# A spectral filter and a low-rank mixer: batch 0's spectra made twice against one filter tile, and its loads reordered

## The chip, the cores and the metric

The kernel runs on one core of one Trainium2 chip. The metric is the time of one execution in device microseconds (us); the time of a kernel is the median of its runs. A profile is one execution taken by the hardware profiler. The engines are PE (matrix multiply, with its weight loads shown as PEld), DVE (vector engine), ACT (scalar engine), POOL (GpSimd) and SP, which here only issues transfers. Transfers issued by POOL can change the number type on the way (x and the filters are float32 in memory and float16 on the core), those issued by SP and ACT do not here.

## What is computed

```python
X = np.fft.rfft(x, axis=1)                  # x: 8 batches, 3136 rows, 256 columns
Y = X * (filt_r + 1j * filt_i)[None]        # 1569 frequencies
x = np.fft.irfft(Y, n=3136, axis=1)
h = x.transpose(0, 2, 1) @ U @ V            # rank 32
u = x + h.transpose(0, 2, 1)
out = u + np.maximum(u @ w_ch1, 0) @ w_ch2  # 256 -> 1024 -> 256
```

## The kernel before

3136 is 64 x 49, and each transform is made in two steps of matrix multiplies: over the 64 (the matrix `w64`, lines named f1), and over the 49 with the twiddle factors in it (tables `t2` forward and `g12` backward, one slice for each of 32 residues, `NS`). Residues are worked on in pairs, `m` from 0 to 15; eight residues make one of four parts (`PARTS`), by which tables and filters are loaded.

The product with the filter. `forward` (L510) puts a pair's spectra into one bank `px` of PSUM: real parts in partitions 0 to 63, imaginary parts in 64 to 127. The filter tile `ft` has two halves along its columns. `load_filters` brings the real filter into partitions 0 to 48 of the first half and the imaginary one into the same partitions of the second. `swap_real` (L221) copies the real filter to partitions 64 to 127, `swap_imag` (L228) copies the imaginary one there with its sign turned. `both_products` (L524) then multiplies `px` with both halves in one DVE instruction of 128x1024; the second product is paired with a second copy of the backward table in which the two halves of the partitions are exchanged (`swap_table`, L190, on POOL; part 0's comes by a transfer of its own, `gs_d`, L247). Batches 2 to 7 use `product` (L533): one instruction of 128x512 and two of 64x512 that read one half of the partitions and write the other, and a sum on POOL.

Batch 0 takes a way of its own that stays on the core: `first_f1` (x with `w64`, from x(0) as it lands), `first_a` (a transpose on PE for each pair, evicted by ACT into the tile `a`), `first_mid` (the loop over the 16 pairs: product on DVE, `back` of the pair before, spectra of the pair two ahead, transpose of the pair three ahead), and then transposes into `e2`. Batches 1 to 7 go through memory: `f1_units(b)` (13 units for a batch, L472, with an eviction each) store to `c1`, `load_a` reads the spectra's input back, `stream` makes the products and stores to `c2`, and `load_e` reads that.

From L712 on, the channel mixer (`mm1`, L712, and `mm2`, L738 or L789) runs group by group in an order written out by hand: `put(slot, ...)` sets beside which slot of it a unit of other work is issued, and each engine works through its instructions in that order. Batch 0 uses the first 48 slots.

The order of transfers around the change, all of POOL's in one queue: x(0) in chunks with `load_rest` (the filters' last rows) behind the first; filter part 0, its tables, then for parts 1 to 3 table `t2`, filters, table `g`, with `swap_table` of the part before in between; then x(1) with U between, V (`vqs`), w1, w2, x(2,0); on POOL then the copies of V into order (`v_order`, L284, 14 of them, 8.56 us together), x(2,1), and the copy of w2 (L837). SP's queue holds small constants and the row `nyq`, and later the stores to `c1` and the loads from it. PSUM has eight banks: x 1, f 1, m 4, o 2.

Matmuls whose result nobody reads stand at three places: `keep_on` (L347: 4 before each bank of `first_f1` up to row 16, 8 before the loop) and `keep_in` (L353: 4 or 14 in each pair of the loop, 6 in two units of batch 1).

Of the kernel before, what the change touches and what calls it, by code (L numbers as in the profile page):

```python
# [13 lines left out]
SEQ = 3136  # L14
# [12 lines left out]
def _consts():  # L27
# [22 lines left out]
    for s in range(NS):  # L50
        for j in range(49):
# [10 lines left out]
            if s:  # L62
                t2[s, :49, j], t2[s, 49:, j] = e.real, -e.imag
                t2[s, :49, 64 + j], t2[s, 49:, 64 + j] = sg * e.imag, sg * e.real
                g[s, j] = np.concatenate([ei.real, ei.imag]) * 2
                g[s, 64 + j] = np.concatenate([-ei.imag, ei.real]) * 2 * sg
            else:
                o = 0 if j < 25 else 49
                t2[s, o:o + 49, j] = e.real
                t2[s, o:o + 49, 64 + j] = e.imag  # L70
                g[s, j, o:o + 49] = ei.real * (2 if f else 1)
                g[s, 64 + j, o:o + 49] = -ei.imag * 2

    t2[0, :, 64] = 0
    t2[0, 49:, 64] = (-1.0) ** r
    g[0, 64] = 0
    g[0, 64, 49:] = (-1.0) ** r
    g *= ESC / n
    gs = np.concatenate([g[:, 64:], g[:, :64]], 1)
# [6 lines left out]
            np.ascontiguousarray(gs[0:8].transpose(1, 0, 2)).astype(f16))  # L86
# [3 lines left out]
def kernel(  # L90
# [13 lines left out]
    w64_np, s2_np, idn_np, fold_np, wp_np, t2_np, g_np, gs_np = _consts()  # L104
# [7 lines left out]
    gs_d = nc.inline_tensor(gs_np, name="gsd")  # L112
# [8 lines left out]
    BUFS = {"x": 1, "f": 1, "m": 4, "o": 2}  # L121

    def bank(tag, name):
        return ps.tile([128, 512], F32, tag=tag, bufs=BUFS[tag], name=name)

# [47 lines left out]
    nyq = sb.tile([128, DM], F32, tag="ocho", bufs=1, name="nyq")  # L173
    PARTS = ((0, 8), (8, 16), (16, 24), (24, 32))
    for a, b in PARTS:
        for c in (0, NS * DM):
            nc.vector.memset(ft[32:64, c + a * DM:c + b * DM], 0.0)  # L177

    def load_table(k, a, b):

        dst, src, w = ((t2, t2_d, 128), (g12, g_d, 98))[k]
        n, p = (b - a) * w, dst.shape[0]
        nc.gpsimd.dma_start(dst[:, a * w:b * w],
                            bass.AP(tensor=src, offset=a // 8 * p * n, ap=[[n, p], [1, n]]))

    def swap_table(a, b):

        o = NS * 98
        for p, q in ((0, 64), (64, 0)):
            nc.gpsimd.tensor_copy(g12[p:p + 64, o + a * 98:o + b * 98],  # L190
                                  g12[q:q + 64, a * 98:b * 98])

    def load_filters(a, b):

        d = max(a, 1)
        for c, src in ((0, filt_r), (NS * DM, filt_i)):
            nc.gpsimd.dma_start(
                ft[0:24, c + a * DM:c + b * DM],
                bass.AP(tensor=src.tensor, offset=a * DM, ap=[[64 * DM, 24], [1, (b - a) * DM]]))
            nc.gpsimd.dma_start(  # L200
                ft[25:49, c + d * DM:c + b * DM].rearrange("p (k d) -> p k d", d=DM),
# [3 lines left out]
    def load_rest():  # L205

        for c, src in ((0, filt_r), (NS * DM, filt_i)):
            nc.gpsimd.dma_start(
                ft[25:49, c:c + DM],
                bass.AP(tensor=src.tensor, offset=32 * DM, ap=[[64 * DM, 24], [1, DM]]))  # L210
            nc.gpsimd.dma_start(
                ft[24:25, c:c + NS * DM],
                bass.AP(tensor=src.tensor, offset=24 * 64 * DM,
                        ap=[[NS * DM, 1], [1, NS * DM]]))
        nc.sync.dma_start(
            nyq[64:65, :],
            bass.AP(tensor=filt_r.tensor, offset=(SEQ // 2) * DM, ap=[[DM, 1], [1, DM]]))

    def swap_real(a, b):

        nc.vector.tensor_copy(ft[64:128, a * DM:b * DM], ft[0:64, a * DM:b * DM])  # L221

    def swap_imag(a, b):

        fb = NS * DM
        if a == 0:
            nc.vector.memset(ft[0:1, fb:fb + DM], 0.0)
        nc.vector.tensor_scalar_mul(ft[64:128, fb + a * DM:fb + b * DM],  # L228
                                    ft[0:64, fb + a * DM:fb + b * DM], -1.0)
# [9 lines left out]
    for k, part in enumerate(PARTS):  # L239
        if k:  # L240
            load_table(0, *part)
        load_filters(*part)
        if k == 0:
            load_table(0, *part)
        load_table(1, *part)
        if k == 0:
            nc.gpsimd.dma_start(g12[:, NS * 98:(NS + 8) * 98], gs_d.ap())  # L247
        if k > 1:
            swap_table(*PARTS[k - 1])
    load_x(1, 0)  # L250
    uq = sb.tile([128, NR * RANK], F16, tag="esb", bufs=2, name="uq")
    nc.vector.memset(uq[64:128, :], 0.0)
    nc.gpsimd.dma_start(uq[0:64, :], moe_U.rearrange("(q r) p -> q (r p)", q=NQ))
    load_x(1, 1)
    swap_table(*PARTS[3])
    load_x(1, 2)
    vqs = []
    for k in range(2):
        v = sb.tile([128, SEQ // 2], F16, tag="xt", bufs=5, name="vq")
        vqs.append(v)  # L260
        nc.gpsimd.dma_start(v[64:96, :], moe_V[:, k * (SEQ // 2):(k + 1) * (SEQ // 2)])
    w1 = cst.tile([128, 2 * 1024], F16)
    for i in range(4):
        nc.gpsimd.dma_start(
            w1[32 * i:32 * i + 32, :].rearrange("p (h c) -> p h c", h=2),
            bass.AP(tensor=moe_w_ch1.tensor, offset=moe_w_ch1.offset + i * 64 * 1024,
                    ap=[[1024, 32], [32 * 1024, 2], [1, 1024]]))
    w2 = cst.tile([128, 8 * DM], F16)
    w2n = sb.tile([128, 8 * DM], F16, tag="esb", bufs=2, name="w2n")
    nc.gpsimd.dma_start(w2n, moe_w_ch2.rearrange("(cc t) e -> cc (t e)", t=8))  # L270
# [6 lines left out]
    def v_order():  # L277

        for r in range(0, NR, 8):
# [8 lines left out]
            yield  # L288

# [60 lines left out]
    def keep_in(tile, n):  # L350

        for _ in range(n):
            nc.tensor.matmul(tile[:, 0:128], w64[:, :], idn[:, :],  # L353
                             start=True, stop=True, skip_group_check=True)

    def first_f1():
        ne = 0
        xs = [st[0]["x"][c] for c in range(len(CH))]
        for r0 in range(0, NH - 1, 4):
            for dh in range(2):  # L360
                keep_on(4 if r0 < 16 else 0)
# [6 lines left out]
                for h in range(2):  # L368
                    dst = atv[:, dh, :, h * NH + r0:h * NH + r0 + 4]
                    src = pa.rearrange("p (r h k) -> p h k r", h=2, k=64)[:, h]  # L370
                    if ne % 2:
                        nc.vector.tensor_copy(dst, src)
                    else:
                        nc.scalar.copy(dst, src)
                    ne += 1
# [21 lines left out]


    def first_mid(fill):
# [21 lines left out]
        def ahead(m, keep=0):  # L421
            return forward(m, st[0]["a"][m // 4], ("m",), keep)

        pxs = [ahead(0), ahead(1)]
        keep_on(8)
        for m in range(NS // 2):
            for k, part in enumerate(PARTS):
                if k and 2 * m == part[0]:
                    swap_real(*part)
                    swap_imag(*part)  # L430
            uv = both_products(m, pxs.pop(0))
            if pend is not None:
                back(*pend)
            pend = (m, uv)
            if m + 2 < NS // 2:
                pxs.append(ahead(m + 2, 4 if m % 4 or not m else 14))
            if m + 3 < NS // 2:
                first_a(m + 3)
            if m >= 12:
                next(fill)  # L440
        prep_u()
        back(*pend)
        e2 = new_e2(0, 0)
        for k4, n0 in enumerate(range(0, NH, 4)):
            pt = ps.tile([128, 1024], F16, tag="m", bufs=BUFS["m"], name="pe")
# [8 lines left out]
            if k4 in (1, 2, 3, 4):  # L454
                next(fill)

    def f1_units(b, both):
        ne = 0
        for c in range(len(CH)):
            xt = st[b]["x"].pop(c)  # L460
            last = b == 1 and c == len(CH) - 1
            if last:
                asb = sb.tile([128, 8 * DM], F16, tag="och", bufs=2, name="asb")
                odd_row = sb.tile([64, DM], F16, tag="ocho", bufs=1, name="asb1")
            else:
                asb = sb.tile([128, 9 * DM], F16, tag="asb", bufs=2, name="asb")
            for n0 in range(0, CH[c], 2):
# [3 lines left out]
                keep_in(pf, 6 if b == 1 and ne in (2, 3) else 0)  # L471
# [3 lines left out]
                if both and (ne % 2 if b > 1 else ne > 3 and ne not in (5, 7, 9, 12)):  # L475
# [464 lines left out]
```

## Time and profile before

| what | value |
|---|---|
| runs | 524.3, 526.23 and 526.81 us (median 526.23) |
| the profiled execution | 523.76 us |
| its span, first to last instruction | 522.0 us |
| PE busy | 496.7 us (95%) |
| DVE busy | 407.7 us (78%) |
| ACT busy | 377.5 us (72%) |
| POOL busy | 301.9 us (58%) |
| first L712 (dense work of PE) | 53.61 us |
| batch 0's products (L524) | 19.98 to 44.16 us |
| batch 1's first product | 64.88 us |

The page lists busy time by engine, the span in 40 slices, the transfers by queue, the chain of waits that ended last, and the costliest groups of instructions. A line of the timeline gives start and length in us, the engine, the line of the code, the operation, what is written from what, the shape and the count of instructions merged into it; in square brackets stands how long the engine was idle before it and what ended that. A line of the windows gives, for a stretch of time, the busy time of PE, PEld, DVE, ACT and POOL (with the number of instructions), the granted clock, the share of the 16 transfer engines in use and the GB/s.

### The profile page before, as it was taken

The page shows a single profiled execution, that of the slowest core. Times are in us where ns is not written, and L with a number is a line of the kernel's source. Part 1 is how long each engine was busy: PE and PEld are TensorE (multiplying, and loading weights), DVE is VectorE, ACT ScalarE, POOL GpSimd, SP SyncE. Part 2 cuts the span into 40 slices and gives each one's busy share as a digit, 9 for nine tenths or more (in the row PEclk, how much of TensorE's full clock was granted, in tenths as well). Part 3 has the DMA queues.
Part 4 walks back from the last instruction along what each step waited for, and adds up shares of the span by engine and source line. Part 5 has one row for each costly group of instructions (what it writes and reads, how often), then busy time and mean ns, then how long its engine had stood idle before and what let it go on. Part 6 is the DMA issues. An engine that isn't in the chain of part 4 may idle for free.

```text
span 522.0 us, 11372 instructions
## 1 busy us (share of the span) xinstructions
PE 496.7 (95%) x3976; PEld 327.4 (63%) x3976; DVE 407.7 (78%) x585; ACT 377.5 (72%) x772; POOL 301.9 (58%) x430
## 2 busy tenths in 40 slices
PE   4878899999989999999999999999999999999997
PEld 3766477777656665666666666666666666555555
DVE  7897386677888888998998888988999877436654
ACT  2767757768778768887788878888777678665552
POOL 7798733445765757775777675965666564313001
PEclk9999999999999999999999999999999999999999
DMA  8989998978899798887898698888777575644325
GB/s 135 188 143 221 233 214 203 213 209 191 197 202 253 180 203 181 215 219 176 235 216 221 162 253 207 184 227 194 180 194 150 129 167 134 139 100 80 71 62 121
DMA packets 122571, 93.99 MB, mean 180 GB/s; under 512 B 58017, under 2 KB 104866, under 8 KB 122514
## 3 DMA queue, kind: packets, MB, share of 16 engines
q1 hardware_dynamic: 98986, 50.93, 39.1%
q0 software_dynamic: 20240, 40.60, 37.9%
q10 hardware_dynamic: 3288, 1.74, 1.3%
q8 instruction: 31, 0.51, 0.4%
q14 instruction: 26, 0.21, 0.1%
HBM read 56.25 MB, written 48.17 MB: 200 GB/s over the span
## 4 chain that ended last, share of the span: by engine, by line
PE 78%; DVE 9%; DMA 6%; POOL 3%; issue 2%; ACT 1%; ACTq 0%; SPq 0%; DVEq 0%; POOLq 0%
PE phh L712 28%; PE po L789 25%; PE px L516 5%; PE pi L552 5%; PE pu L637 4%; PE po L738 4%; DVE uv L537 4%; DMA xt<-in_x_dram 3%; PE pf L472 3%; PE ph L594 2%; DVE ft L177 1%; DVE uv L535 1%; DMA out_dram<-och 1%; DMA g<-gd 1%; DMA a<-c 1%
## 5 line engine op out<-in xcount | busy, mean ns | idle before, releaser
L720 ACT ACTIVATE h<-phh 128x512 f16<-128x512 f32 (+1 forms) x391 | 205.4, 578 | 68.6 <-PE phh L712 64.1
L712 PE MATMUL phh<-ut,w 128*128 128x512 f16 x768 | 197.5, 379 | 0.3 <-ACT h L720 0.3
L540 POOL TENSOR_TENSOR y<-uv 128x512 f16<-128x512 f16 x96 | 111.8, 1165 | 100.1 <-DVE uv L537 80.3
L789 PE MATMUL po<-h,w 128*128 128x512 f16 x656 | 168.5, 379 | 0.0
L712 PEld LDWEIGHTS <-w 128*128 128x128 f16 x832 | 114.2, 144 | 54.5 <-issue 0.9
L537 DVE TENSOR_TENSOR uv<-px,ft 64x512 f16<-64x512 f32 x192 | 132.1, 688 | 2.6
L807 POOL DMA_DIRECT2D out_dram<-och x148 | 85.9, 588 | 81.6 <-DVE och L799 38.9
L789 PEld LDWEIGHTS <-w 128*128 128x128 f16 x656 | 60.5, 98 | 57.8 <-issue 1.1
L535 DVE TENSOR_TENSOR uv<-px,ft 128x512 f16<-128x512 f32 x96 | 64.9, 676 | 35.2 <-PE px L516 33.0
L556 ACT CAST esb<-pi 98x512 f16<-98x512 f32 x112 | 65.9, 589 | 32.1 <-PE pi L552 28.2
L798 DVE TENSOR_TENSOR tt<-po,ut 128x512 f32<-128x512 f32 x82 | 56.7, 692 | 34.3 <-PE po L789 32.3
L799 DVE STREAM_TRANSPOSE och<-tt 128x512 f32<-128x512 f32 x82 | 58.4, 712 | 2.8
L516 PE MATMUL px<-a,t 98*128 98x256 f16 x256 | 49.1, 273 | 5.6 <-DVE uv L537 2.8
L478 ACT CAST asb<-pf 128x512 f16<-128x512 f32 (+1 forms) x80 | 46.1, 576 | 6.5 <-PE pf L472 3.8
L524 DVE TENSOR_TENSOR uv<-px,ft 128x1024 f16<-128x1024 f32 x32 | 38.0, 1219 | 11.7 <-PE px L516 11.2
L702 ACT CAST ut<-pu 128x512 f16<-128x512 f32 x82 | 44.8, 612 | 0.0
L516 PEld LDWEIGHTS <-t 98*128 98x128 f16 x256 | 22.7, 98 | 31.6 <-DVE uv L537 10.6
L552 PE MATMUL pi<-y,g 128*98 128x256 f16 x192 | 36.7, 272 | 0.1
L472 PE MATMUL pf<-xt,w 128*128 128x512 f16 (+1 forms) x91 | 33.2, 370 | 1.0 <-DMA xt<-in_x_dram 1.0
L738 PE MATMUL po<-w,h 128*128 128x256 f16 x256 | 33.2, 273 | 0.0
L552 PEld LDWEIGHTS <-g 128*98 128x98 f16 x256 | 29.6, 123 | 3.2 <-issue 0.8
L637 PEld LDWEIGHTS <-e 96*128 96x128 f16 x686 | 26.4, 98 | 7.2
(99 smaller groups left out, 420.0 us busy)
## 6 DMA issues: line engine op xcount, KB each, us to landing
xt<-in_x_dram POOLq DMA_DIRECT2D x46, 256.0 KB, 6.6
out_dram<-och SPq DMA_DIRECT2D x180, 64.0 KB
a<-c SPq DMA_DIRECT2D x28, 384.0 KB
e<-c SPq DMA_DIRECT2D x56, 192.0 KB
out_dram<-och POOLq DMA_DIRECT2D x148, 64.0 KB, 3.5
c<-esb SPq DMA_DIRECT2D x24, 384.0 KB
c<-asb POOLq DMA_DIRECT2D x30, 256.0 KB, 5.6
out_dram<-och POOLq DMA_DIRECT2D x12, 256.0 KB, 4.8
```

Source lines behind the costliest of these rows:

```text
L516: nc.tensor.matmul(px[:, sl * DM:(sl + 1) * DM], t2[:, s * 128:(s + 1) * 128], a2[:, (2 * ml + sl) * DM:(2 * ml + sl + 1) * DM], start=Tru ...
L535: nc.vector.tensor_mul(uv[:, 0:512], px[:, :], ft[:, a:a + 512])
L537: nc.vector.tensor_mul(uv[p:p + 64, 512:1024], px[q:q + 64, :], ft[q:q + 64, b:b + 512])
L540: nc.gpsimd.tensor_add(y, uv[:, 0:512], uv[:, 512:1024])
L552: nc.tensor.matmul(pi[0:98, sl * DM:(sl + 1) * DM], g12[:, g:g + 98], y[:, o:o + DM], start=(fi == 0), stop=(fi == nf - 1), skip_group_che ...
L556: nc.scalar.copy(split(esb[:, ml * 512:(ml + 1) * 512]), natural(pi[0:98, :]))
L712: nc.tensor.matmul(pm[:, 0:w], w1[:, dh * 1024:(dh + 1) * 1024].rearrange("p (c t) -> p t c", t=8)[:, t], ut[:, dh * w:(dh + 1) * w], star ...
L720: nc.scalar.activation(h[:, 0:w], pm[:, 0:w], RELU)
L789: nc.tensor.matmul(po[:, :], w2[:, t * DM + dh * 128:t * DM + (dh + 1) * 128], hs[gx, t][:, :], start=(t == 0), stop=(t == 7))
L798: nc.vector.tensor_add(tt, po[:, :], uts[gx][:, dh * 512:(dh + 1) * 512])
L799: nc.vector.transpose(och.rearrange("p (j h a) -> p h j a", h=2, a=32)[:, dh], tt.rearrange("p (j t) -> p j t", t=32))
L807: (nc.gpsimd if k and (b < nb - 1 or r0 > 12) else nc.sync).dma_start(dst, och[32 * i:32 * i + 32, k * 512:(k + 1) * 512] .rearrange("p (r ...
```

## The change

The filter tile. The real filter goes to partitions 0 to 63 of the first half and the imaginary one to 64 to 127, so that one transfer layout is enough for batch 0. The spectra of batch 0 are made twice, eight narrow matmuls for a pair (64 columns of weights each, at column position 0 or 64) into two banks: one bank has the real parts in both halves of the partitions, the other the imaginary parts. One product of 128x1024 then reads the same 512 filter columns for both banks. The real and the imaginary filter are spread for the later batches by three copies for each part (`spread_filters`), twelve in all, placed after the loop. The sign that `swap_imag` turned moves into a table for batch 0 and 1 (`gn_d`, the negated first half) and for batches 2 to 7 into a multiply with -1.0 within one of the two products. The Nyquist row (`nyq`) becomes a 50th frequency of residue 0.

```diff
+        def ahead(m):
+            px = pm[-1].tile([128, 1024], F32, tag="px", bufs=2, name="px")
+            for fi in range(2):
+                for sl in range(2):
+                    s, o = 2 * m + sl, fi * 512 + sl * DM
+                    for q in (0, 64):
+                        nc.tensor.matmul(
+                            px[q:q + 64, o:o + DM], t2[:, s * 128 + fi * 64:s * 128 + fi * 64 + 64],
+                            st[0]["a"][m // 4][:, s % KG * DM:(s % KG + 1) * DM],
+                            start=True, stop=True, tile_position=(0, q), skip_group_check=True)
+            return px
...
+                uv = sb.tile([128, 1024], F16, tag="uv", bufs=3, name="uv")
+                fap = ft[:, 2 * m * DM:2 * (m + 1) * DM]
+                nc.vector.tensor_mul(
+                    uv.rearrange("p (f e) -> p f e", f=2),
+                    pxs.pop(0).rearrange("p (f e) -> p f e", f=2),
+                    bass.AP(tensor=fap.tensor, offset=fap.offset, ap=[fap.ap[0], [0, 2], [1, 512]]))
...
-        for p, q in ((0, 64), (64, 0)):
-            nc.vector.tensor_mul(uv[p:p + 64, 512:1024], px[q:q + 64, :],
-                                 ft[q:q + 64, b:b + 512])
+        nc.vector.scalar_tensor_tensor(uv[0:64, 512:1024], px[64:128, :], -1.0, ft[64:128, b:b + 512],
+                                       op0=mybir.AluOpType.mult, op1=mybir.AluOpType.mult)
+        nc.vector.tensor_mul(uv[64:128, 512:1024], px[0:64, :], ft[0:64, b:b + 512])
...
+    def spread_filters():
+        for a, b in PARTS:
+            lo, hi = slice(a * DM, b * DM), slice((NS + a) * DM, (NS + b) * DM)
+            for dst, src in ((ft[0:64, hi], ft[64:128, lo]), (ft[64:128, hi], ft[64:128, lo]),
+                             (ft[64:128, lo], ft[0:64, lo])):
+                nc.vector.tensor_copy(dst, src)
+                yield
```

The loads. Table part 0 stays on POOL's queue, now ahead of filter part 0. Parts 1 to 3 of `t2`, `g` and the new negated table go to SP's queue, each behind a two-byte transfer (`mark`) that reads what batch 0 has just made, so that they start at row 20 of `first_f1` and at the first transposes of parts 1 and 2. POOL copies only one half of a table part (`swap_table`), for part 0 too. Filter parts 2 and 3 are issued ahead of the table copies of parts 1 to 3; x(1,0), x(1,1) come behind the copy of part 2, x(1,2), V, w1, w2 and x(2,0) behind that of part 3. Only four of the seven steps of `v_order` and the copy of w2 stand ahead of x(2,1), which also waits on a one-element copy on POOL of the last row that `f1_units(1)` evicts.

```diff
+    def tables_behind(k, ap):
+        nc.sync.dma_start(mark[:, k:k + 1], ap)
+        for t in range(3):
+            load_table(t, *PARTS[k], eng=nc.sync)
+
+    load_table(0, *PARTS[0])
+    load_filters(*PARTS[0])
+    load_table(1, *PARTS[0])
+    load_table(2, *PARTS[0])
...
+    load_filters(*PARTS[1])
+    swap_table(*PARTS[0])
+    for k in (2, 3):
+        load_filters(*PARTS[k])
+
+    def loads(k):
+        swap_table(*PARTS[k])
+        if k == 1:
+            nc.gpsimd.dma_start(uq[0:64, :], moe_U.rearrange("(q r) p -> q (r p)", q=NQ))
+        elif k == 2:
+            load_x(1, 0)
+            load_x(1, 1)
+        else:
+            load_x(1, 2)
...
+        if ml == 0 and gi in (1, 2):
+            tables_behind(gi + 1, st[0]["a"][gi][0:1, 0:1])
+            loads(gi + 1)
+            if gi == 2:
+                st[0]["order"] = load_weights()
...
+    nc.gpsimd.tensor_copy(mark[:, 0:1], st[1]["end"][0:1, 0:1])
+    load_x(2, 1)
+    for _ in st[0]["order"]:
+        pass
```

The order of units and the unread matmuls. `first_f1` gets 18, 4, 8, 4, 24, 3, 3, 3, 2, 0, 0, 0 unread matmuls ahead of its twelve banks, and 7 stand behind it and 7 ahead of the loop; those inside the loop and inside batch 1's units go. ACT evicts one bank of `first_f1` and DVE the next, in place of half a bank each. In the loop the transpose of the pair three ahead comes before the spectra of the pair two ahead. One unit of `f1_units(1)` stands in the loop where four stood, two behind it, and five in place of four between the transposes into `e2`. The banks of tag m are taken by pools of their own (`four_banks`), since the loop uses them as two pairs.

```diff
-                keep_on(4 if r0 < 16 else 0)
+                keep_on(next(gaps))
...
-                    if ne % 2:
-                        nc.vector.tensor_copy(dst, src)
-                    else:
-                        nc.scalar.copy(dst, src)
-                    ne += 1
+                    (nc.vector.tensor_copy if dh else nc.scalar.copy)(dst, src)
...
-            if m >= 12:
-                next(fill)
+                if m == NS // 2 - 1:
+                    next(fill)
...
-            if k4 in (1, 2, 3, 4):
+            if k4 in (0, 2, 3, 4, 5):
                 next(fill)
+            if k4 == 6:
+                next(spread)
...
+    for k in range(10):
+        put(k, spread)
```

## The prediction

> **What bounds the kernel now.** I read the page's slices first, for where an engine is not full.
>
> ```profile
> PE   4878899999989999999999999999999999999997
> DVE  7897386677888888998998888988999877436654
> DMA  8989998978899798887898698888777575644325
> ```
>
> One digit is 13 us. From the fourth slice on PE is at 8 or 9 up to the last, so later work can only be moved as a block; DMA is between 7 and 9 for the first 130 us. This change touches the first 65 us and one DVE operation of the later batches. So next, the timeline of the start.
>
> ```profile
> 14.53 2.34 PE L366 MATMUL pa<-w,xt 128*128 128x128 f16 x20
> 17.91 0.69 DVE L221 COPY ft<-ft 64x2048 f16<-64x2048 f16 x1
> 19.98 4.62 DVE L524 TENSOR_TENSOR uv<-px,ft 128x1024 f16<-128x1024 f32 x4
> 24.63 0.69 DVE L221 COPY ft<-ft 64x2048 f16<-64x2048 f16 x1
> 25.05 2.22 POOL L190 COPY g<-g 64x784 f16<-64x784 f16 x2 [0.69 <-DMA g<-gd]
> 25.24 1.32 DVE L228 TENSOR_SCALAR ft<-ft 64x2048 f16<-64x2048 f16 x1
> 26.67 4.62 DVE L524 TENSOR_TENSOR uv<-px,ft 128x1024 f16<-128x1024 f32 x4
> 33.50 4.62 DVE L524 TENSOR_TENSOR uv<-px,ft 128x1024 f16<-128x1024 f32 x4
> 39.55 4.61 DVE L524 TENSOR_TENSOR uv<-px,ft 128x1024 f16<-128x1024 f32 x4
> 49.66 1.29 PE L594 MATMUL ph<-e,usb 128*32 128x256 f16 x25
> 50.88 0.11 PEld L472 LDWEIGHTS <-w 128*128 128x128 f16 x2 [0.49 <-issue]
> 57.74 0.38 PE L472 MATMUL pf<-xt,w 128*128 128x512 f16 x1 [0.71 <-DMA xt<-in_x_dram]
> 62.78 0.39 PE L472 MATMUL pf<-xt,w 128*128 128x512 f16 x1 [0.27 <-DMA xt<-in_x_dram]
> 64.45 0.39 PE L516 MATMUL px<-a,t 98*128 98x256 f16 x2 [0.29 <-DMA a<-c]
> ```
>
> Batch 0's sixteen products run on DVE in four blocks of four, 4.62 us each, from 19.98 to 44.16. Between the blocks DVE spreads filters (L221, L228) for 2.05, 2.21 and 1.43 us; L228 takes 1.32 instead of 0.69 where POOL's L190 runs beside it. The last three lines are the only waits of PE for data after its dense work starts at 53.6 (first L712): x(2,0), x(2,1) and the first part of batch 1's spectra land just when they are wanted. The transfers are therefore the second limit. Third view, windows:
>
> ```profile
> 26.00:28.00 2.00, 0.64 (x10) 0.48 (x8) 1.90 (x3) 0.67 (x2) 1.96 (x4) 1.00 0.56 98
> 28.00:30.00 2.00, 2.00 (x32) 1.78 (x33) 2.00 (x2) 1.37 (x5) 2.00 (x4) 1.00 0.63 152
> 30.00:32.00 2.00, 1.90 (x35) 1.76 (x34) 1.97 (x3) 1.51 (x5) 1.92 (x4) 1.00 0.91 113
> 32.00:34.00 2.00, 1.27 (x21) 1.11 (x18) 1.90 (x3) 1.35 (x4) 2.00 (x3) 1.00 0.60 141
> 34.00:36.00 2.00, 1.22 (x20) 1.12 (x21) 2.00 (x3) 0.55 (x2) 1.96 (x5) 1.00 0.84 114
> 36.00:38.00 2.00, 1.85 (x31) 1.59 (x32) 2.00 (x2) 1.69 (x5) 1.96 (x3) 1.00 1.12 211
> ```
>
> The last but one number is the share of the DMA engines in use. From 26 to 36 us it is short of full by 0.44, 0.37, 0.09, 0.40 and 0.16 of 2 us each: 2.9 us of unused transfer time, while POOL (second last busy column before the clock, 2.00 of 2.00) issues or copies tables. From 36 on it is full.
>
> **The change, part by part.**
>
> *Up to the first product.* x(0)'s last transfer still lands near 15.2, and the unread matmuls (18, 4, 8, 4, 24 and so on) stand where PE waits for x, so they cost nothing there. The L366 row shows 0.117 us for a matmul of 128 columns; L451, the same width, takes 1.07 us for 16, or 0.067. If the filled waits bring the faster pace before 14.5, the 20 matmuls lose about 1 us; ScalarE's evictions (five of 0.47 and one of 0.75 behind 14.9) leave at most 0.7 of it. The first spread, L221 to L828, ends at 19.87, 0.1 before the first product; it is gone from there, and the rest of that wait was for the spectra. I take 0.9 us earlier (bounds 0 and 1.5): product 0 at 19.1.
>
> *The loop of products.* The three spreads in it, 2.05 + 2.21 + 1.43 = 5.7 us of DVE, go. In exchange PE makes the spectra twice: per pair eight matmuls 64 columns wide in place of two of 128, two side by side. L594 is the row nearest: 49 matmuls of 256 columns, four side by side, take 1.52 us in the chain of waits (12.25 groups of 0.109, L738's pace, are 1.33, so 0.19 is left for going into the narrow form and back). So four pairs are 0.44 + 0.19 = 0.63. With the return transform (8 x 98 columns, 0.36 between its starts) and the transpose (4 x 0.055 = 0.22), PE needs 1.21 us per pair; DVE needs 1.15. The unread matmuls that stood here (4 or 14 per pair) go. Sixteen pairs at 1.21 are 19.4 instead of 24.2, 4.8 us saved. Bounds: 18.5 (DVE's pace) and 23 (no two side by side: 1.65 x 13 with some slack).
>
> A rule speaks against this part: the Trainium skill, TensorEngine Tiling (Array Packing), Key Properties, says that a change of the tiling mode drains the TensorE. The trace agrees, with 0.19 us for both ways; by a drain as long as the 0.49 us behind L594 at 50.88, each way, a pair would take 2.0 us and the loop 32, later than before.
>
> The new first return transform waits for POOL's copy of table part 0, which came by its own DMA before: g lands at about 18.7 and the copy takes 0.84 to 1.2 (L190), so 20.3, against a want at 20.3. Parts 1 to 3 of the tables move from POOL's queue to SP's, each gated; filter part 1 should land about 24.2 where its product wants it at 23.9. I charge 0.5 for these. The loop ends at 19.1 + 19.4 + 0.5 = 39.0, against 44.16.
>
> *From the loop to the first dense matmul.* Only one of the 13 units of batch 1's first transform stays in the loop, where four stood; three more evictions of 0.69 fall on DVE before the first L712, where DVE had about 1 us idle (1.00 ahead of L452): +1.0. L712 starts at 49.4 instead of 53.6: 4.2 us ahead.
>
> *Transfers.* 2.9 us of idle time can be filled, since filter part 3 and x(1) are issued ahead of the table copies. Added: the swapped half of the tables, 98 KB for each of four parts where one of 196 KB stood, or 196 KB more, about 1.1 us by the L183 rows (196 KB land 1.08 apart). Nine table transfers leave POOL, whose issue takes 0.57 each. So whatever is bound by transfers comes 1.8 to 2.9 us earlier; x(2,0) lands at 55 to 56 instead of 57.6, while PE would want it at 53.5.
>
> *The late spreads and the gate.* Twelve copies of 0.69 (8.3 us of DVE) are moved between 47 and 60. Ten stand between L712's start and batch 1's first product, where DVE is busy 3.36 of 11.68 us, so 8.3 us are free and 6.9 needed. x(2,1) waits on POOL behind two w2 copies (1.04 each), eight V copies (8.56/14 = 0.61) and the last eviction of batch 1; in the kernel before it stood behind fourteen V copies. Behind x(2,1) only V copies wait that are wanted a group later. I take its landing as unchanged relative to x(2,0).
>
> *The later batches.* One of the two L537 products becomes a multiply with a constant and a product in one instruction. No row shows that operation. Lower bound 0.676 (L535, same elements per partition), upper 1.22 (L524, twice the elements, as if it made two passes). I take 0.69, since 64 or 128 partitions make no difference and elements do: 0 us, hidden behind PE, as DVE is busy 291 of 340 us between 100 and 440.
>
> **Sum.** PE's dense work is ready 4.2 us earlier and the transfers 1.8 to 2.9; PE then waits at x(2,0), and part of that comes back since batch 1's spectra (wait of 0.29) are stored earlier. I take 3.0 us (bounds 1.8 and 4.2). The profiled execution took 523.76 us with a span of 522.0; it becomes 520.8. It was 2.5 us under the median of the runs shown, 526.23, so the median is forecast at 523.2, 0.6% less. About 0.5% (2.6 us) is what a measurement of this kernel can tell from no change.
>
> **Rivals.**
>
> 1. *The front's whole gain is kept.* x(2,0) comes in time because the tables move faster on SP's queue than on POOL's. For it: c1's stores on SP's queue pass x at 54 to 58. Against: DMA is full from 36 on. 5.2 us at the loop's end less little: 521.0. Chance 0.17.
> 2. *The transfers hide it.* x(2,0) and x(2,1) land as before, since the idle time is filled by the added tables and by batch 1's loads from c1, which now come early enough to compete with x(2,0). Gain 0 to 1.5: 525.5. For it: 57.74 and 62.78 above wait for exactly these. Chance 0.24.
> 3. *Slower: DVE and POOL take turns.* At 25.24, L228 was held 0.63 us by L190, and L190's second copy took 1.21 instead of 0.84. The ten late spreads meet ten copies on POOL (0.61 to 1.04). If each waits 0.35 on the other, x(2,1)'s issue moves from 57 to 60.5, and it lands 6.2 us later (as now) at 66.7, where PE stands at it: 62.78 becomes 66.7, +3.9, 530. It decides once the issue is later than 59.2. Against: POOL stands waiting for w2 first, and DVE has that time free. Chance 0.13.
> 4. *The combined product makes two passes.* 96 x 0.53 = 51 us on DVE, which has 49 free between 100 and 440: it would just become the bound, with waits of some 8 us: 531. Chance 0.05. The Trainium skill, Vector Engine (DVE) Microarchitecture Reference, Points that are easy to get wrong, says that this form halves its throughput with two non-bf16 SBUF sources; here one source is PSUM, and no run yet shows it.
>
> **How the numbers follow.** The forecast has 0.41. Faster by over 0.5%: most of the forecast's upper half and rival 1, 0.50. Within 0.5%: the forecast's lower part and rival 2, 0.31. Slower: rivals 3 and 4 and a tail of rival 2, 0.19. The forecast's own range is 521.5 to 525; the full one, which reaches to rivals 1 and 3, is 519 to 529.
>
> **What would show it.** Right: sixteen products without a spread between them, at 1.2 us each, ending near 39; the first dense matmul near 49.4; a wait of 2 us or so for x(2,0) on PE; the combined product at 0.69. Wrong: products 2 us apart (PE's narrow form), a return transform held by POOL's copy, spreads of over 1 us beside V copies with x(2,1) landing after 64, or DVE near full after 100 us.

## The result: 1.1% slower, and the profile after

The changed kernel takes 530.74 us (median of 6 runs, 529.33 to 532.34), the kernel before 525.97 beside it (6 runs, 523.73 to 526.88): a measured ratio of 1.0111, 95% interval 1.0077 to 1.0144 (the two medians alone give 1.009). The forecast was 523.2 with a range of 519 to 529: the wrong sign, and outside the range. The profiled execution took 530.51 us with a span of 528.6 (before: 523.76 and 522.0).

The page's slices of the kernel after; a digit is 13.2 us:

```profile
PE   5799589999999998999999999999999999999996
PEclk9799879999999999999999999999999999999999
DMA  8989886997999796887979699896786674654335
```

PE's fifth slice (53 to 66 us) is at 5, where the kernel before had 8, and the granted clock, whole before behind 17 us, has dips in the second slice and in the fifth and sixth. The timeline of the same stretches, PE and DVE (start, us, engine, line, operation, count, and in brackets the idle time before with what ended it):

```profile
11.38 0.38 PE L379 MATMUL pa<-w,xt 128*128 128x128 f16 x4 [1.72 <-DMA xt<-in_x_dram]
14.99 1.05 PE L379 MATMUL pa<-w,xt 128*128 128x128 f16 x16 [1.80 <-DMA xt<-in_x_dram]
20.53 2.36 DVE L455 TENSOR_TENSOR uv<-px,ft 128x1024 f16<-128x1024 f32 x2 [3.40 <-DMA ft<-in_filt_i_dram]
23.61 1.23 DVE L455 TENSOR_TENSOR uv<-px,ft 128x1024 f16<-128x1024 f32 x1 [0.72 <-PE px L443]
25.19 15.96 DVE L455 TENSOR_TENSOR uv<-px,ft 128x1024 f16<-128x1024 f32 x13 [0.36 <-PE px L443]
...
56.77 0.39 PE L503 MATMUL pf<-xt,w 128*128 128x512 f16 x1 [2.35 <-DMA xt<-in_x_dram]
58.24 0.45 PE L676 MATMUL pu<-s,e 128*128 128x128 f16 x4 [0.54 <-DVE h L748]
62.58 1.07 PE L742 MATMUL phh<-ut,w 128*128 128x512 f16 x4 [0.21 <-ACT h L750]
67.80 0.58 PE L503 MATMUL pf<-xt,w 128*128 128x512 f16 x1 [4.14 <-DMA xt<-in_x_dram]
68.17 1.91 PE L768 MATMUL po<-w,h 128*128 128x256 f16 x8
70.09 0.63 PE L546 MATMUL px<-a,t 98*128 98x256 f16 x2
```

The loop does what it was made for: sixteen products from 20.53 to 41.15, without a spread between them (before: 19.98 to 44.16). The first dense matmul is at 50.99, 2.62 us ahead. Then PE stands 2.35 us for x(2,0) and 4.14 us for x(2,1), where the kernel before stood 0.71 and 0.27. The matmul that started at 62.78 before starts at 67.80 now, 5.0 late, and what is behind it runs at half the clock (1.91 us for eight of L768, where before L738 took 1.04): 6.17 late at 75, and 6.3 at the end. So the loss against this trace is made between 51 and 72 us. Behind that the two seem to keep step, but each has one more long wait of PE, first the kernel before, then the kernel after, here with the row of POOL that belongs to it:

```profile
153.49 0.38 PE L516 MATMUL px<-a,t 98*128 98x256 f16 x2 [1.53 <-issue]
```

```profile
205.73 0.38 PE L582 MATMUL pi<-y,g 128*98 128x256 f16 x2 [1.40 <-POOL y L570]
202.19 2.31 POOL L837 DMA_DIRECT2D out_dram<-och  x4 [4.45 <-DVE ocho L781]
```

The first is, at this length, in that one trace alone. The second, which makes PE 1.56 us later, is in all ten traces that have the change in them (the kernel after and nine of the experiments, at 200 to 207 us) and in none of the three that have the front of the kernel before. So it belongs to the change: POOL's sum `y` (L570), for which PE waits, stands behind four output stores that POOL issues only at 202.19. Why those come later than before is not shown, and no run takes the wait away.

POOL and DVE between 52 and 61 us, from the timelines of the kernel after:

```profile
52.16 2.48 POOL L306 COPY w<-w2n 128x1024 f16<-128x1024 f16 x2 [3.06 <-DMA w2n<-in_moe_w_ch_dram]
54.70 4.00 POOL L281 COPY low<-vq 32x256 f16<-32x256 f16 x4
58.75 0.56 POOL L875 COPY mark<-asb 1x1 f16<-1x1 f16 x1
59.25 1.17 POOL L159 DMA_DIRECT2D xt<-in_x_dram  x2
```

```profile
52.74 4.72 DVE L224 COPY ft<-ft 64x2048 f16<-64x2048 f16 x4
57.49 0.69 DVE L748 TENSOR_SCALAR h<-phh 128x512 f16<-128x512 f32 x1
```

Four V copies take 4.00 us (before: fourteen in 8.56), and the four spreads beside them and beside the copies of w2 take 4.72 instead of 4 x 0.69: the two engines take turns. Ahead of that POOL stands 3.06 us for w2n, which lands at 52.04, since the copies of w2 are now in front of x(2,1) and were behind it before. x(2,1) is issued at 59.25 and 59.82, where before it was at 56.01 and 56.58. The windows (PE, PEld, DVE, ACT, POOL busy with counts, clock, DMA share, GB/s) show what the transfers did meanwhile, first before, then after:

```profile
56.00:58.00 2.00, 1.29 (x7) 0.54 (x6) 0.69 (x1) 1.84 (x4) 1.96 (x4) 1.00 0.94 281
58.00:60.00 2.00, 2.00 (x15) 1.07 (x14) 0.33 (x1) 1.78 (x4) 1.24 (x2) 1.00 1.03 180
```

```profile
30.00:32.00 2.00, 2.00 (x36) 1.62 (x36) 1.98 (x3) 1.59 (x5) 0.12 (x1) 1.00 0.40 109
32.00:34.00 2.00, 2.00 (x35) 1.53 (x35) 1.98 (x3) 1.80 (x6) 2.00 (x4) 1.00 0.73 230
...
56.00:58.00 2.00, 0.93 (x6) 0.51 (x7) 1.94 (x3) 0.81 (x2) 2.00 (x3) 1.00 0.20 67
58.00:60.00 2.00, 1.76 (x8) 0.62 (x8) 1.42 (x3) 0.91 (x2) 1.96 (x5) 0.60 0.43 129
60.00:62.00 2.00, 2.00 (x7) 0.81 (x6) 1.94 (x3) 1.24 (x3) 1.96 (x3) 0.54 1.10 246
```

Between 56 and 60 us, where PE is about to need x(2,1), the transfers stand idle for 2 x 0.80 + 2 x 0.57 = 2.7 us: POOL, which has to issue it, is copying. And once it is issued, its queue moves nothing until 62.1 us: batch 1's loads from c1 (`a<-c`, issued on SP from 57.81) fill the DMA engines. By queue, in busy share of the 16 engines:

```
us            POOL's queue   SP's queue
58.0 to 60.0      0.00          0.42
60.0 to 62.0      0.00          1.08
62.0 to 64.0      0.55          0.59
64.0 to 66.0      0.58          0.58
```

So x(2,1)'s halves land at 66.05 and 67.66, 6.8 and 7.8 us behind their issues.

### The profile page after: what moved, and what is told of

Same layout as the page of the kernel before. It is cut to its first block, busy times and chain, and to the rows that moved or that the text cites. A ratio compares the mean times of both kernels' runs of the same rounds, so it can differ in the third digit from the quotient of the medians.

```text
span 528.6 us, 11468 instructions
## 1 busy us (share of the span) xinstructions
PE 502.6 (95%) x4017; PEld 328.2 (62%) x4017; DVE 414.5 (78%) x590; ACT 376.0 (71%) x769; POOL 299.6 (57%) x423
## 4 chain that ended last, share of the span: by engine, by line
PE 80%; DMA 7%; DVE 6%; POOL 4%; issue 1%; ACT 1%; SPq 0%; ACTq 0%; POOLq 0%; DVEq 0%
PE phh L742 28%; PE po L819 25%; PE pi L582 5%; PE px L546 5%; DMA xt<-in_x_dram 4%; PE po L768 4%; PE pu L667 4%; PE pf L503 3%; PE ph L624 2%; DVE uv L568 2%; DMA w2n<-in_moe_w_ch_dram 2%; PE px L443 1%; DVE uv L566 1%; DVE uv L565 1%; POOL xt L159 1%
## 5 line engine op out<-in xcount | busy, mean ns | idle before, releaser
L750 ACT ACTIVATE h<-phh 128x512 f16<-128x512 f32 (+1 forms) x391 | 206.1, 578 | 69.9 <-PE phh L742 65.1
L570 POOL TENSOR_TENSOR y<-uv 128x512 f16<-128x512 f16 x96 | 111.9, 1166 | 100.2 <-DVE uv L568 86.3
L819 PEld LDWEIGHTS <-w 128*128 128x128 f16 x656 | 60.5, 98 | 57.9 <-issue 1.1
L566 DVE SCALAR_TENSOR_TENSOR uv<-px,ft 64x512 f16<-64x512 f32 x96 | 66.5, 693 | 1.3
L568 DVE TENSOR_TENSOR uv<-px,ft 64x512 f16<-64x512 f32 x96 | 65.6, 684 | 1.3
L509 ACT CAST asb<-pf 128x512 f16<-128x512 f32 (+1 forms) x77 | 44.4, 576 | 13.5 <-PE pf L503 11.0
L546 PE MATMUL px<-a,t 98*128 98x256 f16 x224 | 43.3, 274 | 2.9 <-DVE uv L568 2.4
L546 PEld LDWEIGHTS <-t 98*128 98x128 f16 x224 | 20.2, 99 | 27.7 <-DVE uv L568 10.1
L768 PE MATMUL po<-w,h 128*128 128x256 f16 x256 | 34.0, 277 | 0.0
L159 POOL DMA_DIRECT2D xt<-in_x_dram x50 | 29.9, 610 | 1.8 <-issue 1.0
```

The source lines that it names most:

```text
L546: nc.tensor.matmul(px[:, sl * DM:(sl + 1) * DM], t2[:, s * 128:(s + 1) * 128], a2[:, (2 * ml + sl) * DM:(2 * ml + sl + 1) * DM], start=Tru ...
L566: nc.vector.scalar_tensor_tensor(uv[0:64, 512:1024], px[64:128, :], -1.0, ft[64:128, b:b + 512], op0=mybir.AluOpType.mult, op1=mybir.AluOp ...
L568: nc.vector.tensor_mul(uv[64:128, 512:1024], px[0:64, :], ft[0:64, b:b + 512])
L570: nc.gpsimd.tensor_add(y, uv[:, 0:512], uv[:, 512:1024])
L750: nc.scalar.activation(h[:, 0:w], pm[:, 0:w], RELU)
L819: nc.tensor.matmul(po[:, :], w2[:, t * DM + dh * 128:t * DM + (dh + 1) * 128], hs[gx, t][:, :], start=(t == 0), stop=(t == 7))
```

## The experiments

Ratios are against the kernel before, run on the same chip in the same session (524.2 to 524.4 us there). The theory at the outset: x(2,1) is issued late, since POOL's copies and DVE's spreads take turns, and that is the loss. Rivals: the half clock; the spreads' load on DVE; the transfers.

### x(2,1) issued early, and the spreads apart

The first is the kernel after with x(2,1) issued behind the first step of the V copies (two copies) and no gate; the second moves the ten late spreads from the first ten slots of the batch-2 order to later ones, apart from each other; the third does both.

```diff
 # e1_x21_early
-    nc.gpsimd.tensor_copy(mark[:, 0:1], st[1]["end"][0:1, 0:1])
-    load_x(2, 1)
...
             next(order)
+            if k == 0:
+                load_x(2, 1)
 # e2_spread_paced
-    for k in range(10):
+    for k in (6, 10, 11, 12, 15, 16, 17, 20, 21, 22):
         put(k, spread)
```

> The changed kernel with x(2,1) issued on POOL right behind the first step of the V copies, without the gate; nothing else moved. Theory A (the late issue of x(2,1), 59.3 us against 56.0, is the loss): it is issued near 48 and lands by 61, the wait of 4.1 us on PE for it goes and with it the second stretch of half clock; the dense work stands about 6 us earlier, the time is 524 to 526, about that of before. Theory B (the transfers are full and an earlier x(2,1) only pushes x(2,0) and batch 1's spectra back): PE waits as long in sum, 529 or more.

> The changed kernel with ten of the twelve filter spreads put at slots 6, 10, 11, 12, 15, 16, 17, 20, 21, 22 instead of 0 to 9, so that few of them meet POOL's copies of w2 and V before x(2,1) is issued. Theory C (DVE and POOL take turns on the path that they share, which delays x(2,1)): the copies take 0.72 and 1.04 us again, x(2,1) is issued near 57.3 instead of 59.3, its wait shrinks by about 2, and the time is near 528.5. Theory D (x(2,1) is late for its place in the queue alone, behind w2): no more than 0.5 us is won, 530.

> Both: x(2,1) early and the spreads paced. If the two are the whole loss, batch 1's first product keeps most of the 2.6 us by which the dense work starts earlier: 522.5 to 524.5. If the transfers set the end, it is no better than x(2,1) early alone.

Measured: x(2,1) early 526.23 us, 1.0029 (1.0001 to 1.0056); spreads paced 527.57, 1.0077 (1.0047 to 1.0107); both 526.64, 1.005 (1.002 to 1.0081). The timeline of PE with x(2,1) early:

```profile
56.44 0.39 PE L505 MATMUL pf<-xt,w 128*128 128x512 f16 x1 [0.94 <-DMA xt<-in_x_dram]
59.14 0.59 PE L678 MATMUL pu<-s,e 128*128 128x128 f16 x4 [1.77 <-DVE h L750]
64.34 0.38 PE L505 MATMUL pf<-xt,w 128*128 128x512 f16 x1
65.54 0.38 PE L548 MATMUL px<-a,t 98*128 98x256 f16 x2
```

The wait of 4.14 us is gone (the third line, nothing in brackets), and with it 0.0111 - 0.0029 = 0.8%, some 4.3 of 5.8 us by the ratios (2.9 of 4.8 by the medians). What is left, 0.3% or 1.5 us, is of the size of the wait at 205 us, which this run has too. A second wait comes forward: 1.77 us for one relu (`h`, L750) that stands on DVE behind four spreads of 4.10 us together. With the spreads paced that wait is gone too, and x(2,1) is issued 1.5 us earlier (57.79) and waited for 1.12 instead of 4.14. So the taking of turns is 1.5 of the 3.2 us by which the issue is late; the rest, the place behind w2, stays. But the spreads now stand between batch 1's products on DVE, and the lateness grows from 0.6 us at 69 us to 2.4 at 94 and 3.2 at the end. By its interval this run can't be told from the kernel after, only from the kernel before; its trace ends 3.1 us sooner. Both edits together give no more than the first.

### Is a late issue dear by itself?

The kernel before with one line moved, and the kernel after with batch 1's loads held on SP until the first half of x(2,1) has landed:

```diff
 # e6_before_x21_late
-    load_x(2, 1)
     for h in range(2):
         nc.gpsimd.tensor_copy(split(w2)[:, :, h], natural(w2n)[:, :, h])
+    load_x(2, 1)
 # e9_c1_held, in load_a
+        if b == 1 and gi == 0:
+            nc.sync.dma_start(mark[:, 1:2], st[2]["x"][1][0:1, 0:1])
```

> The kernel before with one line moved: x(2,1) is issued behind the copies of w2 and not ahead of them. Theory 1 (the late issue of x(2,1) is by itself what costs): it is issued near 59 instead of 56.0, lands near 64 to 66 instead of 61.3 and 62.7, PE waits 2 to 4 us for it at the second half of batch 2's first unit, and the time is 528 to 530, a ratio of 1.005 to 1.008. Rival (the loss of the kernel after needs its late spreads beside POOL's copies): PE waits under 1 us for x(2,1) and the time stays within 0.3% of the kernel before.

> The kernel after with batch 1's loads of its intermediate array (a<-c) held on SP until the first half of x(2,1) has landed; x(2,1) is issued as late as in the kernel after. Theory 1 (what makes the late issue dear is that these loads, on the hardware queue, are in front of x(2,1)): issued near 59.3, x(2,1) lands at 63 to 64.5, 4 to 5 us behind its issue as in the kernel before with the late issue, in place of 66.05 and 67.66; PE waits for it about 1 us in place of 4.14; a part comes back as a wait of 1 to 2 us for the held loads; the time is 528 to 529. Rival (the queue order is nothing, the transfers are just full): x(2,1) lands at 66 or later though it is alone, and the time is 530.7 or more.

Late in the kernel before: 524.68 us, 1.0006 (0.9981 to 1.0032), no difference, so the theory as it was written there is wrong. Held loads: 529.81 (4 runs), 1.0115 (1.0081 to 1.0149), as slow as the kernel after. PE of the two, at x(2,1) and at the first of batch 1's spectra:

```profile
64.41 0.39 PE L472 MATMUL pf<-xt,w 128*128 128x512 f16 x1 [1.34 <-DMA xt<-in_x_dram]
66.24 0.38 PE L516 MATMUL px<-a,t 98*128 98x256 f16 x2 [0.46 <-DMA a<-c]
```

```profile
65.38 0.38 PE L503 MATMUL pf<-xt,w 128*128 128x512 f16 x1 [0.84 <-DMA xt<-in_x_dram]
68.50 0.39 PE L548 MATMUL px<-a,t 98*128 98x256 f16 x2 [1.76 <-DMA a<-c]
```

The wait in the first is 1.34 us, less than the 2 to 4 expected. What decides how long x(2,1) takes is which of the two is issued first, x(2,1) on POOL or the loads from c1 on SP. The table has the issue of x(2,1)'s first half, the first issue of the loads, when x(2,1)'s second half landed and how long after its own issue that was, all in us:

```
kernel             x(2,1) issued   a<-c from   2nd half lands   behind its issue
before                 56.0          59.7          62.7              6.2
late, in before        58.7          60.1          64.4              5.1
spreads paced          57.8          58.7          63.3              5.0
loads held             59.6          64.5          65.2              5.1
after                  59.2          57.8          67.7              7.8
unread before x        59.8          58.2          68.8              8.4
first phase filled     59.3          57.6          67.7              7.7
```

In every kernel where the loads come first, x(2,1) takes 2.6 us longer or more than in the three late ones where it comes first (the kernel before is another case: there x(2,0), in the same queue, landed only at 57.6). In the kernel after the loads come first because the front is ahead: batch 1's intermediate array is stored earlier and read earlier. So the late landing needs two things, the late issue and the front's lead. Holding the loads gives x(2,1) its 5 us back and takes the wait to 0.84, as expected; but PE then waits 1.76 for the held loads, the trace's loss falls only from 6.3 to 4.5 us, and the four runs show no gain that could be told from none. The 2.7 us in which the transfers did nothing are not won back by their order. With x(2,1) early they are used (POOL's queue has 0.68 of the transfer engines from 56 to 58 us), and that is the one edit that wins most of the time back. So the issue of x(2,1) is shown as the cause of most of the loss; that the time, and not only the landing, needs the loads from c1 in front as well is argued.

### The half clock

36 and 60 unread matmuls ahead of the two units that wait for x(2,0) and x(2,1):

```diff
                 pf = bank("o" if b == 1 else "m", "pf")
+                for _ in range({0: 36, 4: 60}.get(ne, 0) if b == 2 else 0):
+                    nc.tensor.matmul(pf[:, 0:128], w64[:, :], idn[:, :],
+                                     start=True, stop=True, skip_group_check=True)
```

> The changed kernel with 36 unread matmuls ahead of batch 2's first unit and 60 ahead of its fifth, where PE waits 2.35 and 4.14 us. Theory E (the half clock behind those waits has a price of its own): the clock stays whole from 24 us on, and the matmuls between 58 and 72 us take half as long; the time falls by 2 to 3.5, to near 528. Theory F (the half clock only fills time in which PE would wait for x(2,1) anyway): under 1 us, 530.

Measured 529.32 us, 1.0104 (1.0073 to 1.0135): no difference from the kernel after. The clock stays whole from 17 to 68.5 us, and PE still waits there:

```profile
62.59 3.51 PE L504 MATMUL pf<-idn,w 128*128 128x128 f16 x60
68.86 0.61 PE L506 MATMUL pf<-xt,w 128*128 128x512 f16 x1 [2.76 <-DMA xt<-in_x_dram]
```

So the slow stretch at 58 to 62 cost nothing: without it PE waits the longer for x(2,1). The one behind 67.8 costs, by the rows, the 1.2 us by which the lateness grows there (5.0 to 6.17); 60 matmuls were too few to keep it away, so no run shows the time without it.

### The front

The kernel after with the first filter phase filled to the end, and the kernel before with the change's unread matmuls alone:

```diff
 # e7_f1_filled
-        gaps = iter([18, 4, 8, 4, 24, 3, 3, 3, 2, 0, 0, 0])
+        gaps = iter([18, 4, 8, 4, 54, 3, 3, 3, 34, 0, 0, 0])
 # e10_before_unread
-                keep_on(4 if r0 < 16 else 0)
+                keep_on(next(gaps))
```

> The kernel after with 30 more unread matmuls in the wait at 11.4 us and 32 more in the one at 15.0 us, so that PE waits in neither. Theory 1: the granted clock stays full between 17 and 24 us, product 0 is at 19.6 or earlier instead of 20.5 and the loop of sixteen products ends 1 to 2 us earlier than 41.15, but x(2,0) and x(2,1) land where they landed (56.7 and 66 to 67.7), so the end moves by less than 1 us: 530 to 531, ratio about 1.010. Rival (the half clock between 17 and 24 us is what costs): the end comes 2 us or more earlier, 528.5 or less.

> The kernel before with one part of the change alone: the numbers of unread matmuls in the first filter phase (18, 4, 8, 4, 24, 3, 3, 3, 2, 0, 0, 0 in place of 4 each and 0 at the end). Theory 1 (what ends that phase is the landing of x, not PE's pace, and behind it the transfers bind): the first product moves by less than 0.5 us from 19.98, and the time stays within 0.3% of the kernel before. The step of the prediction (the faster pace brings the first product 0.9 us earlier): it is at 19.1, and the time is about 0.9 us less.

Measured: 530.17 us, 1.0108 (1.0075 to 1.014); and 525.75, 1.0027 (0.9997 to 1.0056). With the phase filled the clock is whole from 7.8 to 65.8 us, yet the first product is at 20.87, not at 19.6, and the first dense matmul only 3.36 instead of 2.62 us ahead; the end does not move. In the kernel before, the unread matmuls alone put the first product at 21.11, 1.1 later than without them.

These two numbers don't show that PE's pace is nothing. The part of x(0) that the last sixteen matmuls of the phase wait for, the last but one, landed later in these executions (15.29 and 16.24, against 14.63 in the kernel before and 14.85 in the kernel after), and in the filled run 34 unread matmuls ran on to 16.19, 0.9 behind that landing. The step from the start of those sixteen matmuls to the first product is free of that. In five traces with the change's front and a whole clock there (x(2,1) early, both, w2n behind, all edits, phase filled) it is 4.67 to 4.69 us. In three with half clock from 16.1 or 17.5 us (the kernel after, spreads paced, loads held) it is 5.54 or 5.55, and in two whose half clock ended at 17.1 and 17.3 it lies between (4.94 and 5.08). PE and DVE with w2n behind, where x(0) landed as in the kernel after:

```profile
14.75 1.05 PE L381 MATMUL pa<-w,xt 128*128 128x128 f16 x16 [1.22 <-DMA xt<-in_x_dram]
19.43 9.36 DVE L457 TENSOR_TENSOR uv<-px,ft 128x1024 f16<-128x1024 f32 x8 [2.54 <-ACT a L409]
```

So the landing of x says when the phase ends, and the half clock behind it costs 0.86 us up to the first product. The filled run shows that this is not what the end waits for: there PE waits 6.43 us for x(2,1).

### Room in the transfers, and a version of all edits

x(2,1) early with w2n's transfer behind x(2,0); the same with 38 unread matmuls ahead of batch 1's first spectra; and the first of these with the front filled and the spreads moved.

```diff
 # e5_w2_behind, with x(2,1) early
-        nc.gpsimd.dma_start(w2n, moe_w_ch2.rearrange("(cc t) e -> cc (t e)", t=8))
         load_x(2, 0)
+        nc.gpsimd.dma_start(w2n, moe_w_ch2.rearrange("(cc t) e -> cc (t e)", t=8))
 # e11_e5_filled, also, ahead of the first product of forward
+        for _ in range(0 if held else 38):
+            nc.tensor.matmul(px[:, 0:128], w64[:, :], idn[:, :],
+                             start=True, stop=True, skip_group_check=True)
 # e8_together: e5, the gaps of e7, and
-    for k in range(10):
+    for k in (0, 1, 4, 5, 6, 7, 11, 12, 16, 17):
```

> The kernel after with x(2,1) issued behind the first V product, as in the run of x(2,1) early, and the transfer of w2n issued behind x(2,0) in place of ahead of it. Theory 1 (the transfers are full until x(2,0), so what is ahead of it in them sets its landing): w2n's bytes move behind x(2,0), which lands near 54 instead of 56.4, its wait of 0.94 us on PE is gone, the w2 copies come at 57 to 60, and the time is near 524, a ratio of about 0.998. Rival (transfers only trade places): x(2,0) still lands at 56 or later, or the first product with w2 waits for the late w2 copies, and the time is 526 or more.

> The kernel with w2n's transfer behind x(2,0), and 38 unread matmuls ahead of batch 1's first forward product, where PE waited 2.66 us for a<-c at 62.86 and then ran at half the granted clock for 3.4 us. Theory 1 (the half clock cost it some 2 us): no half clock behind 62 us, the stretch between 63 and 69 us about 2 us shorter, and the time 525 to 526 in place of 527.6. Rival (batch 1's products on DVE, or the transfers, set the pace there): the clock is whole and the time stays at 527 to 528.

> The kernel after with three edits: x(2,1) behind the first V product and w2n behind x(2,0), as in the run of w2n behind; the two waits of the first filter phase filled with 62 more unread matmuls; and the ten late spreads at slots 0, 1, 4, 5, 6, 7, 11, 12, 16 and 17 of the batch-2 order, not at the first ten. Theory 1 (each of the three is a separate loss): the first product near 19.6, x(2,0) near 54, no wait over 1 us between 50 and 70 us, and the time 521 to 523.5, a ratio of 0.991 to 0.996. Rival (the transfers or DVE bind behind x(2,1) whatever is done in front): the time is that of the kernel before or more, 525 to 527.

Measured: 527.61 us, 1.0056 (1.0033 to 1.0079); 526.92, 1.0045 (1.001 to 1.0081); 526.42, 1.0043 (1.002 to 1.0067). None is faster than the kernel before, and they can't be told from x(2,1) early. PE in the first:

```profile
53.02 0.38 PE L505 MATMUL pf<-xt,w 128*128 128x512 f16 x1
58.84 0.38 PE L505 MATMUL pf<-xt,w 128*128 128x512 f16 x1
62.86 0.38 PE L548 MATMUL px<-a,t 98*128 98x256 f16 x2 [2.66 <-DMA a<-c]
64.94 0.63 PE L505 MATMUL pf<-xt,w 128*128 128x512 f16 x1
65.37 1.91 PE L770 MATMUL po<-w,h 128*128 128x256 f16 x8
```

x(2,0) now lands at 50.87 (56.72 in the kernel after), more than expected, and PE passes both x's without a wait, its first dense matmul 3.9 us ahead. But it then waits 2.66 us for batch 1's spectra. Their way through c1 has become the limit: the last store is issued at 52.64 and the first load at 58.88, 6.2 us later (4.0 in the kernel before, 55.70 to 59.70), while POOL's queue (w2n up to 54.38, then x(2,1)) takes about half of the transfers (queue shares of 0.71 and 0.39 at 54 to 56 us, 0.44 and 0.46 at 56 to 58). Then comes half clock. With the 38 unread matmuls the clock stays whole from 17 us to the end, and the wait is still 1.68 after them; the median is 0.1% better, less than its interval. With all edits two waits stand, 1.05 for x(2,1) at 60.53 and 2.80 for batch 1's spectra at 64.69, and its first product is at 21.64, not 19.6. The profiled run of the first kernel is the lowest of its ten (524.85); what the slower ones wait for is open.

## Why the prediction was wrong, by its own steps

- *The late spreads and the gate* is the step that failed: "I take its landing as unchanged relative to x(2,0)". It went from 5.1 us behind x(2,0) (57.61, 62.74) to 10.9 (56.72, 67.66). The copies on POOL were counted, but not that those of w2 can't start before w2n has landed at 52.04, which kept POOL idle for 3.06 us. The V copies were costed at 0.61 and took 0.72 to 1.19 beside the spreads; these were costed at 0.69 and took 1.00 to 1.43 there. And the loads from c1, which the front's own lead brings forward, were not looked for on SP's queue.
- *Rival 3* (0.13) was the outcome: issue at 60.5 (59.25), landing at 66.7 (67.66), 530 (530.7). That 530 came so close is in part luck: the issue was earlier than it said and the landing took 7.8 us where it said 6.2, and the wait at 205 us is in no sum. The full range was said to reach to this rival, but ended at 529. The rival's reason was half of it. The issue was at 59.25; in the kernel before one at 58.74 cost 1.1 us more of wait and nothing that can be measured, and with the loads from c1 out of the way one at 59.62 brought the wait down to 0.84. Late and behind those loads, PE waits 4.
- *Up to the first product*: 0.9 earlier was forecast; it came 0.55 later. The faster pace came at 7.2 us and emptied the 24 unread matmuls in 1.50 us, so PE waited 1.72 and 1.80 us all the same; from 17.45 to 24.28 the clock was half. This is the sentence "so they cost nothing there": the half clock took 0.86 us (5.55 for 4.69 from the phase's last sixteen matmuls to the first product). With a whole clock the product would have come at 14.99 + 4.69 = 19.7, an estimate from these rows, so the faster pace was mis-sized as well: 0.3 earlier, not 0.9.
- *The loop*: 1.23 us per pair for 1.21 (15.96 / 13), 41.15 for 39.0 at the end; of the difference 1.4 is the first product, and the loop itself took 20.6 for 19.9, with two gaps of 0.72 and 0.36 where 0.5 had been charged. The price of the narrow form, 0.19 for both ways, fits the pace; a drain of 0.49 each way, with 2.0 us a pair, is excluded.
- *From the loop to the first dense matmul*: 2.62 ahead for 4.2: the loop's 2.15 less, and 0.6 back, since only 0.4 of the 1.0 charged was lost.
- *Transfers*: 1.8 to 2.9 us earlier was forecast, x(2,0) came 0.9 earlier, which is no more than it moves from one execution to the next (56.5 to 58.2 us in the three traces with the front of before). The idle time was not filled: from 26 to 36 us the shares are 0.93, 0.98, 0.40, 0.73 and 0.94, 2.0 us unused for 2.9, and 16 to 20 us (0.67 and 0.76) has 1.1 us that were in use before. Rival 2 had the gain hidden too, but because the idle time would be full; what fits of it is that the loads from c1 come early enough to compete, with x(2,1) and not with x(2,0). (In the window rows that the prediction reads here, POOL is the last of the busy columns, not the second last.)
- *The later batches*: the price was right, the "0 us" was not. L566 takes 0.693 us for the 0.69 forecast, and DVE is busy 290 us between 100 and 440 where it was 291. But PE loses 1.56 us at 205 us in every trace with the change. In the lateness, 6.17 at 75 and 6.3 at the end, this is hidden by the 1.53 us that the trace of before lost at 153. The rival by the Trainium skill's page (Vector Engine (DVE) Microarchitecture Reference, Points that are easy to get wrong: half the throughput with two non-bf16 SBUF sources) did not come about; one source is PSUM here.
- Windows, chain and rivals were weighed one at a time; the late landing came from two of them together, a lead and a late issue.

## What to carry to other kernels

Here a stretch that is bound by transfers gave a faster front nothing, since the transfer that PE wanted next was not issued earlier with it; look first at who issues such a transfer and what stands in front of it there. When something runs earlier, list what it triggers on the other queues: here the lead brought other loads ahead of the one that was waited for. Copies that were put "in free time" on DVE cost POOL time as well (1.5 us here), and a DMA on POOL's queue waited behind them. And one pair of traces that agree at the end can still hide a loss: compare the lateness along the way, over several traces.

## What the runs showed of the hardware

- POOL's and SP's transfers share the DMA engines. With SP's queue empty or nearly so, a load on POOL's queue began to move 1.3 us behind its issue (58.74 to 60.0; 59.62 to 60.9). With SP's queue already full it moved nothing for 2.9 us (59.25 to 62.1; two other traces 2.9 and 3.4) and had half of the engines from there on. Why it got nothing at first, though it later shares evenly, is open. In those three traces spreads ran on DVE at that time (60.52 to 62.88 in the kernel after); with the loads held they began only when the transfer had (61.03), so they are not excluded.
- The half clock came in stretches of 3.41 or 6.83 us, and it came without any long wait: in the kernel after from 17.45 us on, with no wait of PE over 1.80 us since the clock had become whole at 7.21, and with x(2,1) early from 59.02 on, with waits of 0.94 and 1.77 at 56 to 59. Waits of the same size were also followed by none: 1.16 and 1.22 us at 12 and 15 us (w2n behind), 1.68 behind 38 unread matmuls. So no length of wait decides it here. The Trainium skill (TensorE: Matmul & The Clock Gate, Part 1) has a window of about 3.4 us, and the lengths here agree with it; it has the clock fall after an idle window, and here it fell with waits of about half that length.
- Side by side, copies of POOL and of DVE within SBUF slowed each other: a V copy on POOL, 0.71 to 0.78 us alone, took up to 1.26, a copy of w2 1.50 for 1.04, and a spread on DVE, 0.69 alone, up to 1.43.
